# Weights decoded by one product, a shift and two merges, with the first two units on VectorE, and new orders in the first and the last head pairs

## The chip, the cores and the metric

The kernel runs on one core of a Trainium2 chip. The metric is the device time of one execution in microseconds (us). The kernel before takes 601.79 us, the median of three runs (601.74 to 602.01). Its profiled execution took 602.28 us. From its first to its last instruction that execution spans 600.4 us.

## The reference

Attention with a soft cap, then two feed-forward layers. In short:

```python
q, k, v: [2, 12, 448, 64] float32          # 2 batches, 12 heads
s = cap * tanh((q @ k.T / 8) / cap)
a = softmax(s) @ v                          # -> x: [896, 768]
h = x @ w_in;  g = h * sigmoid(1.702 * h);  y = g @ w_out      # 768 -> 2048 -> 768
yn = y / sqrt(mean(y*y) + 1e-6) * rms_g
out = (silu(yn @ w_gate) * (yn @ w_val)) @ w_out2              # 768 -> 1536 -> 768
```

The five weight matrices are float64. The kernel therefore reads each weight as two 32-bit words, `lo` and `hi`, and makes the float32 number from them on the chip. The float64 exponent has 11 bits and a bias of 1023, the float32 exponent has 8 bits and a bias of 127.

## The kernel before

**Arithmetic.** Every matrix product whose precision matters is made of three: a number is split into a high part that TensorE takes in its fast format (float32r) and the rest, and the products high-high, high-rest and rest-high are added in PSUM.

**Attention.** There are 12 *pairs* of heads, p = 0 to 11. A pair has three full key chunks (c = 0, 1, 2) for both heads, and one chunk of the last 64 keys of both heads together (c = 3, "last"). Per pair:

- VectorE splits q and k (`split_kq`, L253 and L254), two pairs ahead.
- TensorE makes the scores (L272, 6 products for each chunk; L280, 3 for the last). A chunk of scores takes one of three PSUM buffers. The last chunk, the outputs and the sums take turns in two others.
- ScalarE takes tanh (L299) and exp (L302), in place, in tiles `pa` (chunks 0, 1) and `pb` (chunks 2, 3).
- TensorE makes the outputs (L318, 32 products of a quarter each) and the sums of the probabilities (L362). The sums are fed by streams: chunk 1 for pairs below 4, then `ts`, which is a sum of two or three chunks, then the last chunk. For pairs below 4 `ts` is one addition on GpSimd (L346); from pair 4 on VectorE adds two chunks first (L340) and GpSimd the third.
- VectorE copies the outputs from PSUM (`copy_out`, L330) and takes the reciprocals of the sums (L367). Both free a PSUM buffer that TensorE needs for the next pair.
- The reciprocals go through DRAM (`keep_recips`, `spread`) and come back spread over the partitions; for the last three pairs a product with `sel` spreads them (L383). Five pairs later VectorE multiplies and splits the result (`norm_mul`, `norm_hi`, `norm_lo`).

The code is written out in the order in which each engine gets its work; nothing else reorders it. In pass p of the loop stand the scores of pair p (chunks 1, 2), then chunk 0 of pair p+1, the last chunk of p, and behind them the outputs and sums of pair p-1.

**Weights.** A *unit* is 128 x 768 weights, and there are 68. SyncE's queue loads a unit's words into `raw` (three buffers); a load for unit w+3 waits until unit w is decoded (`low`). Unit by unit, `open_`, then the decoding, then a split into two parts in `ring` (`high_part`, `low_part`). From unit 2 on ScalarE makes a mask in three instructions (`square`, `sign`, `mask`), VectorE puts the exponent and mantissa under it (`mid`), merges the sign and top bits (`top`) and the three bits of `lo` (`low`). Units 0 and 1 are decoded during attention: ScalarE takes the absolute value (`size`), VectorE limits it and shifts (`clip`, `field`), then `top` and `low`; `plan_a` and `plan_d` say in which pass each of these stands.

**Feed-forward.** Columns of 18 products (`group`, L580 to L582) run unit by unit, and `tick` and `ahead` place the decoding of later units behind them. All eight PSUM banks then belong to one pool, so the first column takes over a bank that attention had used.

Of the kernel before, what the change touches and what calls it, by code (L numbers as in the profile page):

```python
# [8 lines left out]
F32 = mybir.dt.float32  # L9
F32R = mybir.dt.float32r  # L10
U32 = mybir.dt.uint32
AF = mybir.ActivationFunctionType
# [5 lines left out]
def attn_moe_kernel(  # L18
# [24 lines left out]
    NC = 3  # L43
# [5 lines left out]
    def f(ap):  # L49
        return ap.bitcast(F32)  # L50
# [1 line left out]
    keep = ctx.enter_context(tc.tile_pool(name="keep", bufs=1))  # L52
    capt = keep.tile([128, 1], F32, name="capt")
    tsc = keep.tile([128, 1], F32, name="tsc")
    edge = keep.tile([128, 1], F32, name="edge")
    blk = keep.tile([128, 128], F32, name="blk")
    ones = keep.tile([128, 128], F32R, name="ones")
    sel = keep.tile([128, 64], F32, name="sel")
# [63 lines left out]
        dec_t[w] = (d, r[:, :, 0], r[:, :, 1])  # L122
        return dec_t[w]

    def size(w):
        d, lo, hi = open_(w)
        nc.scalar.activation(out=f(d), in_=f(hi), func=AF.Abs)

    def clip(w):
        d = dec_t[w][0]  # L130
        nc.vector.tensor_scalar(out=f(d), in0=f(d), scalar1=2.0 ** -15, scalar2=None, op0=ALU.max)

    def field(w):
        d = dec_t[w][0]
        nc.vector.tensor_scalar(
            out=d, in0=d, scalar1=3, scalar2=0x3FFFFFFF, op0=ALU.logical_shift_left, op1=ALU.bitwise_and
        )

    def square(w):
        d, lo, hi = open_(w)  # L140
        nc.scalar.activation(out=f(d), in_=f(hi), func=AF.Square, scale=2.0 ** 15)  # L141

    def sign(w):
        d = dec_t[w][0]
        nc.scalar.activation(out=f(d), in_=f(d), func=AF.Sign, bias=edge)  # L145

    def mask(w):
        d = dec_t[w][0]
        nc.scalar.activation(out=f(d), in_=f(d), func=AF.Relu, scale=2.0 - 2.0 ** -23)  # L149

    def mid(w):
        d, lo, hi = dec_t[w]
        nc.vector.scalar_tensor_tensor(  # L153
            out=d, in0=hi, scalar=3, in1=d, op0=ALU.logical_shift_left, op1=ALU.bitwise_and
        )

    def top(w):
        d, lo, hi = dec_t[w]
        nc.vector.scalar_tensor_tensor(  # L159
            out=d, in0=hi, scalar=0xC0000000, in1=d, op0=ALU.bitwise_and, op1=ALU.bitwise_or  # L160
        )

    def low(w):
# [7 lines left out]
    def high_part(w):  # L171
        ring = pools["ring0" if w % 6 < 3 else "ring1"]
        t = ring.tile([128, 2, 768], F32R, tag="ring", name="ring")
        nc.scalar.activation(out=t[:, 0], in_=f(dec_t[w][0]), func=AF.Copy)  # L174
        wt[w] = t

    def low_part(w):
# [5 lines left out]
            done.add((op, w))  # L183
            op(w)

    ACT_OPS, DVE_OPS = (square, sign, mask), (mid, top, low)

    def block(u0, i):
        w = wt[u0 + i // 6]
# [3 lines left out]
    def attention():  # L193
        with ExitStack() as actx:
# [145 lines left out]
                nc.vector.tensor_tensor(out=ts_[p], in0=pa[p][:, 0], in1=pa[p][:, 1], op=ALU.add)  # L340

            def add_third(p):
                eng = nc.gpsimd if p < NPR - 1 else nc.vector
                if p < THREE:
                    ts_[p] = ap_.tile([128, 2, S], F32, tag="ts", name="ts")
                eng.tensor_tensor(  # L346
                    out=ts_[p], in0=pa[p][:, 0] if p < THREE else ts_[p], in1=pb[p][:, 0:2], op=ALU.add
                )

            def sums(p):  # L350
                ps = ps_v.tile([128, 512], F32, tag="v", name="v")
                streams = [pa[p][:, 1]] if p < THREE else []
                streams += [ts_[p], None]
# [12 lines left out]
                nr[p] = zrp.tile([128, SH], F32, tag="rs", name="rs", bufs=4)  # L366
                nc.vector.reciprocal(out=nr[p], in_=ps[:, 0:SH])  # L367
# [73 lines left out]
            plan_a = {  # L441
                1: [(size, 0)], 2: [(size, 1)], 3: [(high_part, 0)], 5: [(high_part, 1)],
                12: [(square, 2), (sign, 2), (mask, 2)],
            }
            plan_d = {
                1: [(clip, 0), (field, 0)], 2: [(top, 0), (low, 0)], 3: [(clip, 1), (field, 1)],
                4: [(low_part, 0), (top, 1)], 5: [(low, 1)], 7: [(low_part, 1)],
            }

            def decode(plan, p):  # L450
# [1 line left out]
                    run(*op)  # L452

            split_first(ts, x)

            for p in range(NPR + 1):
                load_kq(p + 3)
# [19 lines left out]
                elif p < NPR:  # L477
                    tanh(p, 0)
                    scores(p, 1)
                    tanh(p, 1)  # L480
                    scores(p, 2)
                    tanh(p, 2)
                    scores(p + 1, 0)
                    scores_last(p)
                    tanh(p, NC)
                    exp(pa[p])
                    exp(pb[p])
                    decode(plan_a, p)
                else:
                    decode(plan_a, p)  # L490
                if 3 <= p < NPR:
# [5 lines left out]
                decode(plan_d, p)  # L497
                if p < NPR:
                    add_two(p)
                if p == 1:  # L500
                    outputs(0, (2, NC))
                elif p:
                    outputs(p - 1)
                if NPR - 1 <= p:
                    spread_late(p - 2)
                if p:
                    if p < NPR:
                        copy_out(p - 1, "D")
                    sums(p - 1)
                    if p < NPR - 2:  # L510
                        keep_recips(p - 1)
                if p < NPR:
                    add_third(p)
                if NPR - 3 <= p < NPR:
# [1 line left out]
                if p == NPR:  # L516
                    copy_out(p - 1, "A")
                    some = (p - 3, p - 2, p - 4)
                    for step in (norm_mul, norm_hi, norm_lo):
                        for q_ in some:  # L520
                            step(q_)
            return spread_product, norm_mul, norm_hi, norm_lo

    def rest(spread_product, norm_mul, norm_hi, norm_lo):
        with ExitStack() as fctx:
# [29 lines left out]
            def ahead(u):  # L555

                return (
                    [(high_part, u + 3), (square, u + 5), (mid, u + 4), (top, u + 4)],
                    [(sign, u + 5), (mask, u + 5), (low, u + 4), (low_part, u + 3)],
                )  # L560


# [63 lines left out]
            for c in range(NC1):  # L626
# [18 lines left out]
                for n, (i, b) in enumerate(order):  # L645
                    last = ()
                    if c == 0 and n == 0:
                        later(lambda: spread_product(q3, [bank()[:, 0:B * S // 4] for _ in range(2)]))
                        later(lambda: norm_mul(q3), lambda: norm_hi(q3), lambda: run(mid, 2), lambda: norm_lo(q3))
# [207 lines left out]
            while due:  # L857
                tick(lambda: None)

    nc.vector.memset(edge, -0.99)  # L860
    nc.vector.memset(f(ones), 1.0)
    with tc.manual_schedule():
        tail = attention()
# [65 lines left out]
```

## Time and profile before

| what | value |
| --- | --- |
| median of three runs | 601.79 us |
| profiled execution, and its span | 602.28 us, 600.4 us |
| TensorE busy (PE) | 586.3 us, 98% |
| VectorE busy (DVE) | 445.7 us, 74% |
| ScalarE busy (ACT) | 388.6 us, 65% |
| GpSimd busy (POOL) | 66.1 us, 11% |
| mean granted TensorE clock | 0.996 of full speed |

"Busy" is time in which an instruction is in the engine. Shares over the whole span mix two stages. Attention fills the first 102 us and the two feed-forward layers the rest. In a timeline a row gives start, length, engine, line, instruction (output <- inputs) and count; a bracket gives the engine's idle time ahead of it and what ended that. An instruction that does not need the one ahead of it on its engine starts a little before that one's end, so lengths overlap by some 0.08 us; the chain of waits counts each stretch of time once.

### The profile page before, as it was taken

The numbers are of one execution on the slowest core, as the hardware profiler recorded it, in microseconds if no ns is written. First come the engines' busy times: TensorE is split into PE (matmuls) and PEld (weight loads), VectorE is DVE, ScalarE is ACT, GpSimd is POOL, SyncE is SP. The second block draws the span as 40 slices with busy tenths as digits, with TensorE's granted clock in tenths as the row PEclk, the third lists the DMA queues.
The fourth block names the chain that finished last, engine by engine and source line by source line (L and its number), as shares of the span: only waits on it lengthen the run. The fifth ranks groups of instructions, "written<-read, shape, count | busy, mean of one in ns | idle before, by whom it ended". The sixth has DMA issues, their size and how long they took to land.

```text
span 600.4 us, 8518 instructions
## 1 busy us (share of the span) xinstructions
PE 586.3 (98%) x3417; PEld 499.9 (83%) x3417; DVE 445.7 (74%) x548; ACT 388.6 (65%) x507; POOL 66.1 (11%) x52
## 2 busy tenths in 40 slices
PE   7899998999999999999999999999999999999997
PEld 4354554898899888888889888899999999999997
DVE  5578998798665446666878899995588896688842
ACT  6989996799756457777667666674455582466400
POOL 1312240000000000000022203200022100122100
PEclk9899999999999999999999999999999999999999
DMA  8265420254342413334324134342333342233012
GB/s 295 99 221 164 144 69 21 87 176 143 119 145 77 149 53 105 106 106 131 121 89 134 60 98 154 110 131 81 101 111 105 106 158 86 73 105 106 1 79 106
DMA packets 54450, 67.93 MB, mean 113 GB/s; under 512 B 2918, under 2 KB 49162, under 8 KB 54410
## 3 DMA queue, kind: packets, MB, share of 16 engines
q1 hardware_dynamic: 54122, 67.15, 34.1%
q8 instruction: 27, 0.44, 0.3%
q10 hardware_dynamic: 288, 0.23, 0.1%
q14 instruction: 13, 0.11, 0.1%
HBM read 64.59 MB, written 2.78 MB: 112 GB/s over the span
## 4 chain that ended last, share of the span: by engine, by line
PE 91%; DVE 4%; ACT 3%; issue 1%; DMA 1%; SPq 0%; DVEq 0%
PE b L582 23%; PE b L581 23%; PE b L580 23%; PE b L790 15%; PE v L318 5%; PE s L272 2%; PE v L362 1%; DVE rs L367 1%; ACT pa L302 1%; PE v L280 1%; ACT pb L302 1%; DMA first<-in_k 1%; ACT pa L299 1%; ACT pb L299 1%; DVE ts L340 1%
## 5 line engine op out<-in xcount | busy, mean ns | idle before, releaser
L580 PE MATMUL b<-x,ring 128*128 128x512 f32 (+1 forms) x480 | 174.0, 362 | 2.2 <-DVE z L401 2.2
L582 PE MATMUL b<-x,ring 128*128 128x512 f32 (+1 forms) x480 | 174.3, 363 | 0.0
L581 PE MATMUL b<-x,ring 128*128 128x512 f32 (+1 forms) x480 | 174.1, 363 | 0.0
L580 PEld LDWEIGHTS b<-x,ring 128*128 128x128 f32 x480 | 90.1, 188 | 12.7 <-DVE z L401 2.6
L581 PEld LDWEIGHTS b<-x,ring 128*128 128x128 f32 x480 | 90.1, 188 | 9.9
L582 PEld LDWEIGHTS b<-x,ring 128*128 128x128 f32 x480 | 90.1, 188 | 9.4
L790 PE MATMUL b<-ring,uA 128*128 128x384 f32 x504 | 87.8, 334 | 0.0
L790 PEld LDWEIGHTS b<-ring,uA 128*128 128x128 f32 x504 | 87.4, 188 | 0.0
L153 DVE SCALAR_TENSOR_TENSOR dec<-raw,dec 128x768 uint32<-128x768 uint32 x66 | 67.8, 1028 | 24.7 <-ACT dec L149 23.4
L159 DVE SCALAR_TENSOR_TENSOR dec<-raw,dec 128x768 uint32<-128x768 uint32 x68 | 73.3, 1077 | 1.1
L179 DVE TENSOR_TENSOR ring<-dec,ring 128x768 fp32r<-128x768 f32 x68 | 66.8, 984 | 4.6 <-ACT ring L174 4.6
L582 PE MATMUL b<-g,ring 128*128 128x384 f32 (+1 forms) x192 | 70.0, 365 | 0.0
L581 PE MATMUL b<-g,ring 128*128 128x384 f32 (+1 forms) x192 | 69.9, 364 | 0.0
L580 PE MATMUL b<-g,ring 128*128 128x384 f32 (+1 forms) x192 | 69.6, 362 | 0.0
L165 DVE SCALAR_TENSOR_TENSOR dec<-raw,dec 128x768 uint32<-128x768 uint32 x68 | 64.9, 955 | 3.7 <-ACT ring L174 2.3
L174 ACT ACTIVATE ring<-dec 128x768 fp32r<-128x768 f32 x68 | 56.7, 834 | 16.4 <-DVE dec L165 8.2
L145 ACT ACTIVATE dec<-dec,edge 128x768 f32<-128x768 f32 x66 | 61.5, 932 | 1.0
L141 ACT ACTIVATE dec<-raw 128x768 f32<-128x768 f32 x66 | 59.2, 897 | 0.5 <-DVE ring L179 0.5
L149 ACT ACTIVATE dec<-dec 128x768 f32<-128x768 f32 x66 | 55.6, 843 | 1.5
L758 POOL TENSOR_TENSOR a<-a,gg 128x512 f32<-128x512 f32 (+1 forms) x18 | 29.6, 1645 | 188.6 <-DVE gg L751 188.6
L761 ACT ACTIVATE uA<-a 128x512 fp32r<-128x512 f32 (+1 forms) x24 | 13.9, 578 | 46.3 <-POOL a L758 34.5
L612 DVE TENSOR_TENSOR g<-gg,g 128x384 fp32r<-128x384 f32 (+1 forms) x32 | 20.0, 625 | 27.3 <-ACT g L609 27.1
(95 smaller groups left out, 640.1 us busy)
## 6 DMA issues: line engine op xcount, KB each, us to landing
raw<-in_moe_w_out SPq DMA_DIRECT2D x20, 768.0 KB
raw<-in_moe_w_in SPq DMA_DIRECT2D x16, 768.0 KB
raw<-in_moe_w_gate SPq DMA_DIRECT2D x12, 768.0 KB
raw<-in_moe_w_val SPq DMA_DIRECT2D x12, 768.0 KB
raw<-in_moe_w_out SPq DMA_DIRECT2D x8, 512.0 KB
v<-in_v SPq DMA_DIRECT2D x12, 256.0 KB
kq<-in_k SPq DMA_DIRECT2D x11, 256.0 KB
kq<-in_q SPq DMA_DIRECT2D x11, 224.0 KB
```

Source lines behind the costliest of these rows:

```text
L141: nc.scalar.activation(out=f(d), in_=f(hi), func=AF.Square, scale=2.0 ** 15)
L145: nc.scalar.activation(out=f(d), in_=f(d), func=AF.Sign, bias=edge)
L149: nc.scalar.activation(out=f(d), in_=f(d), func=AF.Relu, scale=2.0 - 2.0 ** -23)
L153: nc.vector.scalar_tensor_tensor(out=d, in0=hi, scalar=3, in1=d, op0=ALU.logical_shift_left, op1=ALU.bitwise_and)
L159: nc.vector.scalar_tensor_tensor(out=d, in0=hi, scalar=0xC0000000, in1=d, op0=ALU.bitwise_and, op1=ALU.bitwise_or)
L165: nc.vector.scalar_tensor_tensor(out=d, in0=lo, scalar=29, in1=d, op0=ALU.logical_shift_right, op1=ALU.bitwise_or)
L174: nc.scalar.activation(out=t[:, 0], in_=f(dec_t[w][0]), func=AF.Copy)
L179: nc.vector.tensor_tensor(out=t[:, 1], in0=f(d), in1=f(t[:, 0]), op=ALU.subtract)
L580: nc.tensor.matmul(out=wide(o, b), lhsT=w0, rhs=x0, start=first, stop=False)
L581: nc.tensor.matmul(out=wide(o, b), lhsT=w0, rhs=x1, start=False, stop=False)
L582: nc.tensor.matmul(out=wide(o, b), lhsT=w1, rhs=x0, start=False, stop=last)
L790: nc.tensor.matmul(out=os_[t][n][:, 0:HW], lhsT=uA[xi][:, i, tok], rhs=w[:, wi, n * HW:(n + 1) * HW], start=(i == 0 and xi == 0 and wi == ...
```

## The change

1. **Decoding.** The `hi` word, read as a float32, is multiplied by 2^-112 (`scale`). Read so, its exponent field is the float64 exponent divided by 8, and 896 = 8 x 112 is the difference of the two biases. Shifted left by three (`shift`) the product holds the float32 exponent and 20 bits of mantissa. `top` merges the sign alone, and `low` the last three bits as before. `square`, `sign`, `mask`, `mid`, `size`, `clip`, `field` and the constant `edge` go.
2. **Units 0 and 1** are scaled, and their high part is copied, on VectorE. ScalarE has no decoding left before pass 12. The passes change: unit 0 in passes 1 and 2, unit 1 in passes 2 to 4 (before: to pass 7).
3. **Passes 1 and 2**: ScalarE takes `exp(pa)` before the last chunk's tanh, and the outputs and sums of the pair before stand ahead of the last chunk's scores and the next pair's chunk 0. VectorE's copy and reciprocal come ahead of `split_kq` and the decoding.
4. **Pair 0** has its sums fed by four streams, without an addition on GpSimd.
5. **Pass 12**: the multiplications of pairs 8 and 9 stand ahead of the last reciprocal.

```diff
+    def scale(w):
         d, lo, hi = open_(w)
+        if w < 2:
+            nc.vector.tensor_scalar(out=f(d), in0=f(hi), scalar1=2.0 ** -112, scalar2=None, op0=ALU.mult)
+        else:
+            nc.scalar.activation(out=f(d), in_=f(hi), func=AF.Copy, scale=2.0 ** -112)
+
+    def shift(w):
         d = dec_t[w][0]
+        nc.vector.tensor_scalar(out=d, in0=d, scalar1=3, scalar2=None, op0=ALU.logical_shift_left)
...
-            out=d, in0=hi, scalar=0xC0000000, in1=d, op0=ALU.bitwise_and, op1=ALU.bitwise_or
+            out=d, in0=hi, scalar=0x80000000, in1=d, op0=ALU.bitwise_and, op1=ALU.bitwise_or
...
-        nc.scalar.activation(out=t[:, 0], in_=f(dec_t[w][0]), func=AF.Copy)
+        if w < 2:
+            nc.vector.tensor_copy(t[:, 0], f(dec_t[w][0]))
+        else:
+            nc.scalar.activation(out=t[:, 0], in_=f(dec_t[w][0]), func=AF.Copy)
...
-    ACT_OPS, DVE_OPS = (square, sign, mask), (mid, top, low)
+    ACT_OPS, DVE_OPS = (scale,), (shift, top, low)
...
-                1: [(clip, 0), (field, 0)], 2: [(top, 0), (low, 0)], 3: [(clip, 1), (field, 1)],
-                4: [(low_part, 0), (top, 1)], 5: [(low, 1)], 7: [(low_part, 1)],
+                1: [(scale, 0), (shift, 0), (top, 0), (low, 0)], 2: [(high_part, 0), (low_part, 0), (scale, 1)],
+                3: [(shift, 1), (top, 1)], 4: [(low, 1), (high_part, 1), (low_part, 1)],
...
-                    [(high_part, u + 3), (square, u + 5), (mid, u + 4), (top, u + 4)],
-                    [(sign, u + 5), (mask, u + 5), (low, u + 4), (low_part, u + 3)],
+                    [(high_part, u + 3), (scale, u + 5), (shift, u + 4), (top, u + 4)],
+                    [(low, u + 4), (low_part, u + 3)],
```

TensorE in pass 1 and the start of pass 2, before: `s` are scores, `v` the buffers of last chunks, outputs and sums.

```order
L272 MATMUL s<-x 128x448 x18
L280 MATMUL v<-x 128x448 x3
L318 MATMUL v<-pb,v 32x448 x8
L362 MATMUL v<-pa,ones 32x224 x4
L362 MATMUL v<-ts,ones 32x224 x4
L362 MATMUL v<-pb,blk 32x224 x4
L272 MATMUL s<-x 128x448 x18
L280 MATMUL v<-x 128x448 x3
L318 MATMUL v<-pa,v 32x448 x8
```

The same place now:

```order
L253 MATMUL s<-x 128x448 x12
L299 MATMUL v<-pb,v 32x448 x8
L347 MATMUL v<-pa,ones 32x224 x8
L347 MATMUL v<-pb,ones 32x224 x4
L347 MATMUL v<-pb,blk 32x224 x4
L261 MATMUL v<-x 128x448 x3
L253 MATMUL s<-x 128x448 x18
L299 MATMUL v<-pa,v 32x448 x8
L299 MATMUL v<-pb,v 32x448 x8
```

The rest of pair 0's outputs (`v<-pb,v`) and its sums (L347) have moved ahead of the last chunk of pair 1 and of chunk 0 of pair 2, and the stream of `ts` is now two streams of `pa` and `pb`.

VectorE in passes 1 and 2, before: `kq` is the raw pair that is split, `z` the copied outputs, `rs` the reciprocals, `dec` and `raw` belong to a weight unit.

```order
L131 TENSOR_SCALAR dec<-dec 128x768
L135 TENSOR_SCALAR dec<-dec 128x768
L330 COPY z<-v 128x448
L367 RECIPROCAL rs<-v 128x224
L253 CAST x<-kq 128x960
L254 TENSOR_TENSOR x<-kq,x 128x960
L159 SCALAR_TENSOR_TENSOR dec<-raw,dec 128x768
L165 SCALAR_TENSOR_TENSOR dec<-raw,dec 128x768
L330 COPY z<-v 128x448
L367 RECIPROCAL rs<-v 128x224
L253 CAST x<-kq 128x960
L254 TENSOR_TENSOR x<-kq,x 128x960
```

The same place now:

```order
L311 COPY z<-v 128x448
L352 RECIPROCAL rs<-v 128x224
L234 CAST x<-kq 128x960
L235 TENSOR_TENSOR x<-kq,x 128x960
L127 TENSOR_SCALAR dec<-raw 128x768
L133 TENSOR_SCALAR dec<-dec 128x768
L137 SCALAR_TENSOR_TENSOR dec<-raw,dec 128x768
L143 SCALAR_TENSOR_TENSOR dec<-raw,dec 128x768
L311 COPY z<-v 128x448
L352 RECIPROCAL rs<-v 128x224
L234 CAST x<-kq 128x960
L235 TENSOR_TENSOR x<-kq,x 128x960
```

The copy and the reciprocal of pair 0 wait for no decoding any more, four instructions of unit 0 stand together behind the split of pair 3, and the copy of pair 1 stands behind these four.

VectorE at the end of attention, before: `late` is a PSUM buffer with spread reciprocals, the product `z<-z,r` is pair 8's.

```order
L410 CAST x_65<-z 128x448
L417 TENSOR_TENSOR x_66<-z,x_65 128x448
L367 RECIPROCAL rs<-v 128x224
L401 TENSOR_TENSOR z<-z,late 128x448 x2
L398 TENSOR_TENSOR z<-z,r 128x448
L417 TENSOR_TENSOR x_66<-z,x_65 128x448 x3
```

The same place now:

```order
L395 CAST x_64<-z 128x448
L402 TENSOR_TENSOR x_65<-z,x_64 128x448
L383 TENSOR_TENSOR z<-z,r 128x448
L386 TENSOR_TENSOR z<-z,late 128x448
L352 RECIPROCAL rs<-v 128x224
L386 TENSOR_TENSOR z<-z,late 128x448
L402 TENSOR_TENSOR x_65<-z,x_64 128x448 x3
```

The products of pair 8 and of pair 9 (the first with `late`) have moved ahead of the last reciprocal, and only that of pair 10 is left behind it.

## Rows read from the trace of the kernel before

**Rows 1.** Windows: stretch, length; busy PE, PEld, DVE, ACT, POOL; PEclk, DMA, GB/s
```profile
13.30:31.20 17.90, 13.62 (x127) 6.34 (x128) 8.43 (x9) 15.52 (x16) 6.47 (x3) 0.90 0.42 143
...
52.15:88.27 36.12, 34.17 (x351) 17.75 (x347) 34.07 (x42) 32.74 (x32) 10.67 (x6) 1.00 0.41 127
...
101.90:597.00 495.10, 495.00 (x2532) 453.06 (x2532) 367.03 (x449) 303.57 (x424) 41.35 (x28) 1.00 0.32 105
```

**Rows 2.** Timeline, 12 to 32 us: start, length, engine, line, instruction, idle before
```profile
12.29 1.42 ACT L302 ACTIVATE pb<-pb,capt 128x1344 f32<-128x1344 f32 x1
...
20.07 2.09 POOL L346 TENSOR_TENSOR ts<-pa,pb 128x896 f32<-128x896 f32 x1 [4.12 <-ACT pb L302]
...
20.83 1.75 DVE L131 TENSOR_SCALAR dec<-dec 128x768 f32<-128x768 f32 x1 [7.77 <-ACT dec L127]
...
22.61 0.56 DVE L135 TENSOR_SCALAR dec<-dec 128x768 uint32<-128x768 uint32 x1
...
23.76 0.88 PE L280 MATMUL v<-x 128*128 128x448 f32 x3 [1.14 <-DVE z L330]
...
25.09 0.60 DVE L253 CAST x<-kq 128x960 fp32r<-128x960 f32 x1
...
25.72 1.16 DVE L254 TENSOR_TENSOR x<-kq,x 128x960 fp32r<-128x960 f32 x1
25.89 0.40 SPq L217 DMA_DIRECT2D kq<-in_k  x1
...
26.79 0.95 DVE L159 SCALAR_TENSOR_TENSOR dec<-raw,dec 128x768 uint32<-128x768 uint32 x1
...
27.78 0.96 DVE L165 SCALAR_TENSOR_TENSOR dec<-raw,dec 128x768 uint32<-128x768 uint32 x1
```

**Rows 3.** Chain that ended last: start, length, engine, tile, line, count
```profile
25.22 4.91 PE v L318 x32
...
31.27 2.02 PE s L272 x18
33.29 0.82 PE v L280 x3
34.10 3.15 PE v L318 x32
37.25 1.13 PE v L362 x24
...
53.70 1.00 DVE ts L340
54.70 0.54 DVE z L330
55.24 1.46 DVE rs L367
...
74.08 0.76 PE v L362 x16
```

**Rows 4.** Timeline, pairs 6 to 11
```profile
52.15 2.39 PE L272 MATMUL s<-x 64*128 64x448 f32 x18
...
52.74 0.96 DVE L165 SCALAR_TENSOR_TENSOR dec<-raw,dec 128x768 uint32<-128x768 uint32 x1 [2.29 <-ACT ring L174]
...
66.86 0.95 DVE L179 TENSOR_TENSOR ring<-dec,ring 128x768 fp32r<-128x768 f32 x1
...
88.27 1.50 PE L272 MATMUL s<-x 64*128 64x448 f32 x12
```

**Rows 5.** Timeline, end of attention and first product behind it
```profile
98.71 0.62 DVE L417 TENSOR_TENSOR x<-z,x 128x448 fp32r<-128x448 f32 x1
...
99.84 1.56 DVE L367 RECIPROCAL rs<-v 128x224 f32<-128x224 f32 x1 [0.51 <-PE v L362]
101.32 1.09 DVE L401 TENSOR_TENSOR z<-z,late 128x448 f32<-128x448 f32 x2
...
101.93 0.44 PE L580 MATMUL b<-x,ring 128*128 128x384 f32 x1 [2.16 <-DVE z L401]
```

More of the change, by code (lines that the diff above doesn't have):

```diff
@@ L54, in attn_moe_kernel @@
     tsc = keep.tile([128, 1], F32, name="tsc")
-    edge = keep.tile([128, 1], F32, name="edge")
     blk = keep.tile([128, 128], F32, name="blk")
@@ L123, in open_ @@
         return dec_t[w]
-    def size(w):
+    def scale(w):
         d, lo, hi = open_(w)
-        nc.scalar.activation(out=f(d), in_=f(hi), func=AF.Abs)
-    def clip(w):
-        d = dec_t[w][0]
[L131 to L155, printed above, removed]
+        if w < 2:
[3 more added lines that the diff above has]
+    def shift(w):
+        d = dec_t[w][0]
+        nc.vector.tensor_scalar(out=d, in0=d, scalar1=3, scalar2=None, op0=ALU.logical_shift_left)
     def top(w):
@@ L342, in add_third @@
             def add_third(p):
+                if p == 0:
+                    return
                 eng = nc.gpsimd if p < NPR - 1 else nc.vector
@@ L351, in sums @@
                 ps = ps_v.tile([128, 512], F32, tag="v", name="v")
-                streams = [pa[p][:, 1]] if p < THREE else []
-                streams += [ts_[p], None]
+                if p == 0:
+                    streams = [pa[p][:, 0], pa[p][:, 1], pb[p][:, 0:2], None]
+                else:
+                    streams = [*([pa[p][:, 1]] if p < THREE else []), ts_[p], None]
                 for n, some in enumerate(streams):
@@ L439, in attention @@
                 nc.tensor.matmul(out=warm[:, 0:S], lhsT=ones, rhs=xA[0][:, 0, 0:S], start=True, stop=True)
[L441 to L444, printed above, removed]
+            plan_a = {12: [(scale, 2)]}
             plan_d = {
-                1: [(clip, 0), (field, 0)], 2: [(top, 0), (low, 0)], 3: [(clip, 1), (field, 1)],
-                4: [(low_part, 0), (top, 1)], 5: [(low, 1)], 7: [(low_part, 1)],
+                1: [(scale, 0), (shift, 0), (top, 0), (low, 0)], 2: [(high_part, 0), (low_part, 0), (scale, 1)],
+                3: [(shift, 1), (top, 1)], 4: [(low, 1), (high_part, 1), (low_part, 1)],
             }
@@ L454, in attention, with products @@
             split_first(ts, x)
+            EARLY = 3
+            def products(p):
+                outputs(p, range(NC + 1) if p else (2, NC))
+                if p + 1 >= NPR - 1:
+                    spread_late(p - 1)
+                if p < NPR - 1:
+                    copy_out(p, "D")
+                sums(p)
             for p in range(NPR + 1):
@@ L482, in attention @@
                     tanh(p, 2)
-                    scores(p + 1, 0)
-                    scores_last(p)
+                    if p < EARLY:
+                        exp(pa[p])
+                        products(p - 1)
+                        scores_last(p)
+                        scores(p + 1, 0)
+                    else:
+                        scores(p + 1, 0)
+                        scores_last(p)
                     tanh(p, NC)
-                    exp(pa[p])
+                    if p >= EARLY:
+                        exp(pa[p])
                     exp(pb[p])
-                    decode(plan_a, p)
                 else:
@@ L499, in attention @@
                     add_two(p)
[L500 to L511, printed above, removed]
+                if p == NPR:
+                    norm_mul(p - 4)
+                    norm_mul(p - 3)
+                if p >= EARLY:
+                    products(p - 1)
+                if 1 <= p < NPR - 2:
+                    keep_recips(p - 1)
                 if p < NPR:
@@ L518, in attention @@
                     some = (p - 3, p - 2, p - 4)
-                    for step in (norm_mul, norm_hi, norm_lo):
+                    norm_mul(p - 2)
+                    for step in (norm_hi, norm_lo):
                         for q_ in some:
@@ L648, in rest @@
                         later(lambda: spread_product(q3, [bank()[:, 0:B * S // 4] for _ in range(2)]))
-                        later(lambda: norm_mul(q3), lambda: norm_hi(q3), lambda: run(mid, 2), lambda: norm_lo(q3))
+                        later(lambda: norm_mul(q3), lambda: norm_hi(q3), lambda: run(shift, 2), lambda: norm_lo(q3))
                         last = (
```

1 line of the change is left out of this document (removed).

## The prediction

> **What bounds the kernel now.** I read the stretches first, then the timeline of the waiting engines, then the chain of waits. From 101.9 us to 597 us TensorE is busy 495.00 of 495.10 us [rows 1]: the feed-forward layers are bound by TensorE alone, and nothing that the change does to ScalarE and VectorE there can win more than 0.1 us. What can be won lies in attention. TensorE idles 4.3 us from 13.3 to 31.2 and 1.95 us from 52.15 to 88.27 [rows 1], and 2.16 us where attention hands over [rows 5]. In the first of these stretches ScalarE is busy 15.5 of 17.9 us [rows 1], and the waits end with VectorE: a last chunk waits 1.14 us for a copy out of PSUM [rows 2] that stood behind `clip` and `field`. The outputs of pair 1 behind these waits then take 4.91 us where those of pair 2 take 3.15 [rows 3]. The granted clock of that stretch is 0.90, so part of it ran at the lower level, 1.2 GHz: 1.76 us more.
>
> TensorE's own work for a pair is 2.02 of scores, 0.82 of last chunk, 3.15 of outputs and 1.13 of sums, 7.12 us; from pair 4 on the sums take 0.76, and a pair 6.75 us [rows 3].
>
> **The early pairs.** Up to exp of pair 0's `pb`, which ends at 12.29 + 1.42 = 13.71 [rows 2], nothing is moved. Now the rest of pair 0's outputs comes next, half of 3.15, then four streams of sums at 1.13/3 each: 13.71 + 1.58 + 1.51, with some 0.1 of hand-offs, and VectorE's reciprocal of pair 0 can start at 16.9. From there VectorE has everything in one row, in the order shown, up to the reciprocal of pair 3, and never has to wait for data that is not long there. The terms:
>
> - 4 reciprocals at 1.46, 3 copies at 0.54, one addition of 1.00 [rows 3]: 8.46.
> - 4 splits, from the start of a cast to the start of what follows, 26.79 - 25.09 = 1.70 [rows 2]: 6.80.
> - 4 merges (`top`, `low`, two units), start to start 27.78 - 26.79 = 0.99 [rows 2]: 3.96.
> - 2 `low_part` at 0.95 [rows 4]: 1.90.
> - 2 `scale`, 2 `shift`, 2 copies into the ring, all with one source of 768 numbers, at the 0.56 of `field` [rows 2]: 3.36.
> - GpSimd's additions for pairs 1, 2 and 3. While one of 2.09 us ran, a `clip` of VectorE took 1.75 us, and it ended 0.42 after GpSimd [rows 2]; its neighbour `field` of the same size took 0.56. So the two engines exclude each other. VectorE has here no gap in which such an addition could hide except beside work from PSUM, so I take 2.09 for each: 6.27.
>
> The sum is 30.75, and the reciprocal of pair 3 ends at 47.65. The outputs of pair 4 need its buffer; 3.15 + 0.76 later, with a hand-off of 0.1, the scores of pair 6 start at 51.7. Before they start at 52.15 [rows 4]. **The gain so far is only 0.45 us**: TensorE's waits move from ScalarE and `clip` to a VectorE that is full. Two of them stay: before the last chunk of pair 2 (its own work done at about 23.9, the copy of pair 1 at 25.8, by the same terms), and before the last chunk of pair 4 (37.6; the copy of pair 2 at 39.0). In the first the clock may fall again, but outputs 2 are done some 4 us before VectorE reaches their copy, which covers 1.76.
>
> On the exclusion the Trainium skill, SBUF — State Buffer, "Who interferes with whom", says that a VectorE instruction with two SBUF inputs, or in a mode that takes two ports, and a GpSimd instruction that reads SBUF hold a shared pair of ports in turn, the later one blocked. It is the rule that speaks most against putting decoding on VectorE beside these additions; the `clip` row agrees, and the 6.27 stands by the row.
>
> ScalarE loses two `size` and two `high_part` in early pairs; it stops being the limit there, and its new order only serves the outputs. SyncE's queue now issues three weight loads together in pass 1, and that of unit 3 waits for `low` of unit 0, at 25.3 by the terms. Behind it stand pair 0's reciprocals and the loads of pair 5; the latter were issued at 25.89 before [rows 2] and come at about 26 now, 7 us before their split: nothing. `scale` reads every second word. If that made it as slow as a merge, 0.96 [rows 2], two of them add 0.8; from below they can't be under 0.56. On this the Trainium skill, VectorE: DVE Perf Modes, "Mode 2×_2P — use both read ports for one tensor", asks for one SBUF source and an even outermost dimension, not for neighbouring words, so by it both keep 0.56 and the sum stays; by the merge's row the time would be 0.8 more. No row here shows the form.
>
> **Pairs 6 to 11.** No decoding is left after pass 4. From 52.15 to 88.27 five pairs take 36.12 us, against 5 x 6.75 = 33.75. The 2.37 are the two places where VectorE was late: `low` of unit 1 waited 2.29 us for ScalarE's `high_part`, and `low_part` of unit 1 took 0.95 [rows 4]. Both go. What is late next is TensorE itself: VectorE was busy 34.07 in this stretch, 32.2 without these two, 6.4 a pair, under 6.75. The scores of pair 11 then start at 51.7 + 33.75 = 85.45, **2.8 us earlier** than 88.27.
>
> **The hand-over.** TensorE is done with attention at 101.93 - 2.16 = 99.77 and waits for the last reciprocal and then for the product that reads `late`, whose bank the first column takes [rows 5]. This product now stands ahead of the reciprocal. The subtraction before it ends at 98.71 + 0.62 = 99.33; two products at 1.09/2 each [rows 5] end at 100.4, and the column starts at 100.5: **1.4 us**. The reciprocal starts 0.6 later than before; its readers are the spread product and the second column, 3 us on.
>
> **Feed-forward.** Three ScalarE instructions and a merge per unit become one and a `shift` of 0.56. TensorE's own work hides it: 0. From above the gain is the 0.1 idle; from below I take one more wait like the longest on VectorE in these rows, 2.16, which no row suggests.
>
> **Sum.** 2.8 + 1.4 = 4.2: 602.28 - 4.2 = 598.1 for the profiled execution, and, as that stands 0.49 over the median, **597.6 us** for the median.
>
> **Rivals.**
>
> *The additions hide (B).* If GpSimd's three additions fall beside copies and reciprocals, 6.27 goes from the chain. TensorE's own work is then the bound: from 16.9 three pairs at 7.12, one at 6.75 and another last chunk and chunk 0 (1.5), so pair 6 starts at 46.5, 5.2 earlier: 592.4. For it: additions run beside reciprocals in later pairs. Against: in passes 1 to 3 they become ready while VectorE is splitting.
>
> *VectorE dearer, and a low clock (C).* `scale` at 0.96 adds 0.8. If the clock falls at the second wait, near pair 4, where no slack covers it, 1.76 more: 597.6 + 2.6 = 600.2. For it: the clock did fall after waits of this kind. Against: those waits were longer together.
>
> *VectorE the bound for good, slower (D).* If each of the six one-source instructions pays as the blocked `clip` does, 1.75, on top of the three blocks, that is 6 x 1.19 = 7.1: pair 6 starts at 58.8, and the time is 604.7. It decides from 4.2 us more on VectorE in passes 1 to 4. Against: GpSimd has only three additions there.
>
> **Chances.** Forecast 0.55 (its own range 596.2 to 599.2), B 0.12, C 0.24, D 0.05, and 0.04 for something else near no change. The measurement can tell 0.2%, 1.2 us, from no change. B and the forecast are faster, of C two thirds, and the rest of C is the same: faster 0.84, same 0.11, slower 0.05. The range of 594.5 to 600.6 leaves out the far half of B, D and what lies beyond C.
>
> **What would show it.** In the changed profile: TensorE's longest waits in early pairs end with VectorE's copy (L311), at 25 to 26 and at 38 to 39 us; one-source decoding instructions at 0.56, some blocked to 2 us or more by GpSimd; pair 6's scores at 51.7; pairs from there at 6.75; the first column 0.7 us behind the last sums and ahead of the last reciprocal's end; from there 495 us to the end of TensorE. I am wrong if pair 6 starts under 49 or over 53, or if TensorE idles over 1 us in the feed-forward layers.

## The result, and the profile after

The changed kernel takes **596.28 us** (median of four runs, 595.70 to 596.45), the kernel before 601.90 beside it. The ratio is 0.990, with an interval of 0.989 to 0.992. The prediction was 597.6 us. Its sign held, and its mechanism in the main; two of its terms had the wrong size, in opposite directions. The experiments then showed something that it had not considered: one part of the change costs two microseconds.

The profiled execution took 596.45 us with a span of 594.7. The stretches of its time, as in [rows 1]:

```profile
core 0: us, PE busy (x) PEld busy (x) DVE busy (x) ACT busy (x) POOL busy (x), PEclk, DMA share, GB/s
13.30:31.20 17.90, 14.57 (x156) 8.25 (x155) 14.38 (x14) 15.42 (x16) 4.13 (x2) 1.00 0.64 208
31.20:50.00 18.80, 18.80 (x207) 9.47 (x207) 18.52 (x23) 17.41 (x17) 5.23 (x3) 1.00 0.63 189
50.00:82.60 32.60, 32.60 (x329) 17.69 (x331) 29.93 (x38) 31.01 (x30) 10.60 (x5) 1.00 0.37 116
96.00:591.20 495.20, 495.00 (x2532) 453.06 (x2532) 340.56 (x449) 198.16 (x294) 38.06 (x28) 1.00 0.33 105
```

From 96 us on TensorE is busy 495.00 of 495.20 us, as it was 495.00 of 495.10 before, while ScalarE's busy time there fell from 303.57 to 198.16 us. From 31.2 us to the end of attention TensorE no longer idles. TensorE's starts at the places of the sum (the last chunk with the longest wait and the scores behind it, the scores of pairs 6 and 11, the first feed-forward column; start, length, and in brackets the wait ahead):

```profile
26.11 0.87 PE L261 MATMUL v<-x 128*128 128x448 f32 x3 [1.81 <-DVE z L311]
26.91 2.10 PE L253 MATMUL s<-x 64*128 64x448 f32 x18
30.05 0.87 PE L253 MATMUL s<-x 64*128 64x448 f32 x6 [1.03 <-ACT pa L280]
49.79 2.11 PE L253 MATMUL s<-x 64*128 64x448 f32 x18
83.49 1.50 PE L253 MATMUL s<-x 64*128 64x448 f32 x12
96.17 0.45 PE L574 MATMUL b<-x,ring 128*128 128x384 f32 x1 [1.17 <-DVE z L386]
```

Before, these were 52.15 for pair 6 and 88.27 for pair 11 [rows 4], and 101.93 for the first column [rows 5]. So the gain is:

| stretch | before | after | gain | predicted |
| --- | --- | --- | --- | --- |
| to the scores of pair 6 | 52.15 | 49.79 | 2.36 | 0.45 |
| pair 6 to pair 11 | 36.12 | 33.70 | 2.42 | 2.37 |
| pair 11 to the first column | 13.66 | 12.68 | 0.98 | 1.4 |
| feed-forward, TensorE busy | 495.00 | 495.00 | 0 | 0 |

VectorE in the early pairs, from the reciprocal of pair 0 to that of pair 3, as far as it shows what GpSimd does to it (L127 is `scale`, L160 `low_part`, L137 `top`):

```profile
17.24 1.56 DVE L352 RECIPROCAL rs<-v 128x224 f32<-128x224 f32 x1 [0.89 <-PE v L347]
20.42 2.50 DVE L127 TENSOR_SCALAR dec<-raw 128x768 f32<-128x768 f32 x1
29.73 2.75 DVE L160 TENSOR_TENSOR ring<-dec,ring 128x768 fp32r<-128x768 f32 x1
32.41 0.55 DVE L127 TENSOR_SCALAR dec<-raw 128x768 f32<-128x768 f32 x1
35.22 0.96 DVE L137 SCALAR_TENSOR_TENSOR dec<-raw,dec 128x768 uint32<-128x768 uint32 x1
36.10 0.62 DVE L311 COPY z<-v 128x448 f32<-128x448 f32 x1
36.63 1.55 DVE L352 RECIPROCAL rs<-v 128x224 f32<-128x224 f32 x1
43.81 1.55 DVE L352 RECIPROCAL rs<-v 128x224 f32<-128x224 f32 x1
```

And GpSimd's three additions in that time:

```profile
20.39 2.11 POOL L329 TENSOR_TENSOR ts<-pa,pb 128x896 f32<-128x896 f32 x1 [18.20 <-ACT pb L283]
29.18 2.48 POOL L329 TENSOR_TENSOR ts<-pa,pb 128x896 f32<-128x896 f32 x1 [6.68 <-ACT pb L283]
35.51 2.65 POOL L329 TENSOR_TENSOR ts<-pa,pb 128x896 f32<-128x896 f32 x1 [3.85 <-issue]
```

Lay the two over each other. The first addition ran from 20.39 to 22.50, and `scale`, which takes 0.55 at 32.41, took 2.50. The second made `low_part` take 2.75 instead of 0.96. The third came while a merge was running: this time GpSimd's row is the long one (2.65), and what VectorE did after the merge, a copy and a reciprocal, both read from PSUM and took no longer than elsewhere.

### The profile page after: what moved, and what is told of

Same layout as the page of the kernel before. It is cut to its first block, busy times and chain, and to the rows that moved or that the text cites. A ratio compares the mean times of both kernels' runs of the same rounds, so it can differ in the third digit from the quotient of the medians.

```text
span 594.7 us, 8421 instructions
## 1 busy us (share of the span) xinstructions
PE 584.2 (98%) x3425; PEld 500.5 (84%) x3425; DVE 421.2 (71%) x549; ACT 278.5 (47%) x371; POOL 61.5 (10%) x51
## 4 chain that ended last, share of the span: by engine, by line
PE 84%; DMA 6%; DVE 6%; issue 1%; ACT 1%; SPq 0%
PE b L576 23%; PE b L575 23%; PE b L574 23%; PE b L784 15%; DMA r<-recs 4%; DMA recs<-rs 1%; DVE rs L352 1%; DVE x L235 1%; DMA first<-in_k 1%; DMA kq<-in_k 1%; DVE x L234 1%; DVE ts L321 1%; DVE z L311 1%; DVE dec L127 1%; DVE z L383 0%
## 5 line engine op out<-in xcount | busy, mean ns | idle before, releaser
L160 DVE TENSOR_TENSOR ring<-dec,ring 128x768 fp32r<-128x768 f32 x68 | 68.6, 1010 | 23.3 <-ACT ring L155 18.2
L137 DVE SCALAR_TENSOR_TENSOR dec<-raw,dec 128x768 uint32<-128x768 uint32 x68 | 73.2, 1076 | 1.2
L155 ACT ACTIVATE ring<-dec 128x768 fp32r<-128x768 f32 x66 | 55.3, 838 | 35.2 <-DVE dec L143 24.3
L143 DVE SCALAR_TENSOR_TENSOR dec<-raw,dec 128x768 uint32<-128x768 uint32 x68 | 64.9, 955 | 1.4
L752 POOL TENSOR_TENSOR a<-a,gg 128x512 f32<-128x512 f32 (+1 forms) x18 | 26.3, 1462 | 191.5 <-DVE gg L745 183.0
L133 DVE TENSOR_SCALAR dec<-dec 128x768 uint32<-128x768 uint32 x68 | 42.4, 624 | 0.0
L575 PEld LDWEIGHTS b<-g,ring 128*128 128x128 f32 x192 | 36.0, 188 | 4.0
L574 PEld LDWEIGHTS b<-g,ring 128*128 128x128 f32 x192 | 36.1, 188 | 4.0
```

Of the source, the lines that this page charges most:

```text
L133: nc.vector.tensor_scalar(out=d, in0=d, scalar1=3, scalar2=None, op0=ALU.logical_shift_left)
L137: nc.vector.scalar_tensor_tensor(out=d, in0=hi, scalar=0x80000000, in1=d, op0=ALU.bitwise_and, op1=ALU.bitwise_or)
L143: nc.vector.scalar_tensor_tensor(out=d, in0=lo, scalar=29, in1=d, op0=ALU.logical_shift_right, op1=ALU.bitwise_or)
L160: nc.vector.tensor_tensor(out=t[:, 1], in0=f(d), in1=f(t[:, 0]), op=ALU.subtract)
L574: nc.tensor.matmul(out=wide(o, b), lhsT=w0, rhs=x0, start=first, stop=False)
L575: nc.tensor.matmul(out=wide(o, b), lhsT=w0, rhs=x1, start=False, stop=False)
```

## The experiments

The theory T: the gain is made in attention alone, in the three places of the table, and VectorE, blocked by GpSimd, is the limit of passes 1 to 4. Rivals: the lighter decoding in the feed-forward layers gives the gain (R1), or the new orders of passes 1 and 2 give nothing, and only the removed waits for ScalarE and `clip` count (R2). The kernel before took 602.1 to 603.1 us in the medians beside these runs, single runs 601.8 to 603.6; ratios are to those. In five of the profiles (runs 2, 7, 8, 11 and 12 below) sixteen of the first products took some 3.35 us instead of 2.01, so starts are compared from the next place that this does not reach.

**1. New decoding in the feed-forward layers only (the kernel before with it).**

```diff
...
-    ACT_OPS, DVE_OPS = (square, sign, mask), (mid, top, low)
+    ACT_OPS, DVE_OPS = (scale,), (shift, top, low)
...
```

> The kernel before, with the new decoding (one product on ScalarE, shift, two merges) for units 2 and later only; everything in attention stays as before except that one unit's first step in pass 12 is one instruction instead of three. Theory T (the whole gain of 5.5 us is made in attention; in the feed-forward stretch TensorE alone is the limit, busy 495.00 of 495.20 us): 601.5 to 602.2 us, scores of pair 6 at 52.15 and of pair 11 at 88.27 as before, ScalarE's busy time down by some 110 us. Rival R1 (the lighter decoding in the feed-forward layers gives the gain or most of it): 596 to 598.5 us.

602.77 us, ratio 1.000 (0.999 to 1.001). That is 0.6 above T's window, but the kernel before was up beside it too (602.90).

**2. The reverse, the changed kernel with the old decoding from unit 2 on.**

> The changed kernel, with the old decoding (square, sign, mask on ScalarE, mid on VectorE) for units 2 and later; attention keeps the new decoding of units 0 and 1 and the new orders. T: 596.0 to 596.8 us, pair 6 at 49.8, feed-forward 495.0 us. R1: 600 to 602 us.

596.74 us, ratio 0.990 (0.989 to 0.991), that of the changed kernel. The stretch from 96 us, first of 1, then of 2:

```profile
96.00:595.00 499.00, 496.84 (x2573) 452.73 (x2566) 343.52 (x453) 198.92 (x295) 38.07 (x28) 1.00 0.32 104
```

```profile
96.00:595.00 499.00, 495.00 (x2532) 453.09 (x2532) 369.00 (x451) 303.52 (x424) 41.07 (x28) 1.00 0.32 106
```

ScalarE is busy 199 us in the one and 304 in the other; in the second, whose feed-forward layers lie wholly in this stretch, TensorE's 495.00 us stay. (In the first it also holds the end of attention. Run 1 keeps the waits of before: 2.6 us for ScalarE, 2.2 at the hand-over.) R1 falls, twice.

**3. The old hand-over.**

```diff
-                if p == NPR:
-                    norm_mul(p - 4)
-                    norm_mul(p - 3)
...
-                    norm_mul(p - 2)
-                    for step in (norm_hi, norm_lo):
+                    for step in (norm_mul, norm_hi, norm_lo):
```

> The changed kernel, with the products of pairs 8 and 9 back behind the last reciprocal in pass 12. T: the hand-over's 1.0 us goes: first feed-forward column some 2.1 us behind the last sums instead of 1.17, 597.0 to 597.6 us; nothing else moves. Rival (the product waits for its DMA of reciprocals anyway, so the place does not matter): within 0.3 us of 596.3.

599.01 us, ratio 0.994 (0.992 to 0.995): more than T's upper end. The waits of TensorE (us in total, times, longest) and the early stretch of the profiled execution (598.17 us):

```profile
PE b L570 <- DVE z L386: 2.2, 1, 2.2
PE v L261 <- DVE z L311: 1.9, 1, 1.9
```

```profile
13.30:31.20 17.90, 15.43 (x156) 8.79 (x152) 14.22 (x14) 15.41 (x16) 3.95 (x2) 0.91 0.60 197
```

```profile
27.09 4.54 PE L253 MATMUL s<-x 64*128 64x448 f32 x24
```

The first column starts 2.16 us behind the sums, not 1.17: the 1.0 is there. The other 0.7 was there at pair 6 already, at 50.49 (0.15 of it a later start). Nothing differs in the code of these passes; but after the wait of 1.85 us for VectorE's copy the granted clock fell, to 0.91 over the stretch, so that part of it ran at 1.2 GHz, and 24 products of scores took 4.54 us where the changed kernel had 2.10 + 0.87 and a wait of 1.03. With the same instructions up to there and the same wait the clock falls in two of the profiled executions (this one, and run 6 with 0.90) and stays at 1.00 in two others (the changed kernel's and run 2's). How often it falls is not known. The profiled execution is the fastest of the five; where the other four, at 598.78 to 599.18, lose 0.6 to 1.0 us more is not shown.

**4. The old order of scores, exp and outputs in passes 1 and 2.**

```diff
-            EARLY = 3
+            EARLY = 1
```

This brings back the order of all three engines: on VectorE too, copy and reciprocal of passes 1 and 2 stand behind the split and the decoding again.

> The changed kernel, with the old order of scores, exp and outputs in passes 1 and 2 (scores of the next pair ahead of the outputs of the pair before); the new decoding on VectorE, the four streams of pair 0 and pass 12 stay. T has VectorE as the limit of early pairs from the first reciprocal on, and the old order makes that reciprocal start at 20 to 21 us instead of 17.2 because the outputs and sums of pair 0 stand behind 3 us of scores: pair 6 at 51.5 to 53, 598 to 600 us. Rival R2 (the orders give nothing; only the removal of the waits for ScalarE and clip counts): 596.0 to 596.8 us, pair 6 at 49.8.

**594.07 us**, ratio 0.986 (0.984 to 0.987): 2.2 us *faster* than the changed kernel. Both expectations missed; T had the sign wrong, and R2, by which the orders are worth nothing, was 2 us off. Pair 6 starts at 47.74. TensorE's waits, VectorE and GpSimd in early pairs:

```profile
PE s L253 <- ACT pa L280: 1.4, 1, 1.4
PE b L574 <- DVE z L386: 0.7, 1, 0.7
```

```profile
14.27 0.56 DVE L127 TENSOR_SCALAR dec<-raw 128x768 f32<-128x768 f32 x1 [1.01 <-DMA raw<-in_moe_w_in]
20.99 1.74 DVE L234 CAST x<-kq 128x960 fp32r<-128x960 f32 x1
25.79 0.62 DVE L311 COPY z<-v 128x448 f32<-128x448 f32 x1
26.93 1.56 DVE L352 RECIPROCAL rs<-v 128x224 f32<-128x224 f32 x1 [0.51 <-PE v L347]
32.91 0.62 DVE L311 COPY z<-v 128x448 f32<-128x448 f32 x1 [1.25 <-PE v L299]
34.04 1.56 DVE L352 RECIPROCAL rs<-v 128x224 f32<-128x224 f32 x1 [0.51 <-PE v L347]
```

```profile
20.10 2.12 POOL L329 TENSOR_TENSOR ts<-pa,pb 128x896 f32<-128x896 f32 x1 [17.90 <-ACT pb L283]
26.31 2.13 POOL L329 TENSOR_TENSOR ts<-pa,pb 128x896 f32<-128x896 f32 x1 [4.10 <-ACT pb L283]
33.48 2.12 POOL L329 TENSOR_TENSOR ts<-pa,pb 128x896 f32<-128x896 f32 x1 [5.04 <-ACT pb L283]
```

Two things differ. In the old order VectorE decodes unit 0 from 14.27 on, when it has nothing else to do, and not behind the first reciprocal. And exp of `pb`, which releases GpSimd, ends a little behind the outputs of the pair before (for the second addition at 26.24 and 25.73), so the second and third addition run beside a reciprocal from PSUM; only the first blocks VectorE, by 1.1 us (a cast of 1.74 instead of 0.60). TensorE waits once, 1.40 us from 13.3 on; in the changed kernel 0.48, 1.81 and 1.03. The difference of 1.92 is nearly the difference of the distance from the scores of pair 1 to those of pair 6 (9.75 to 47.74, and 10.00 to 49.79: 1.80).

**5. No addition on GpSimd for pairs 1 and 2** (four streams instead of three).

```diff
+            FOUR = 3
...
-                if p == 0:
+                if p < FOUR:
```

> The changed kernel, with the sums of pairs 1 and 2 fed by four streams as those of pair 0, so that GpSimd's two additions at 20.39 and 29.18 us, beside which a product took 2.50 us and a subtraction 2.75 us on VectorE, are not there. Theory T (VectorE, blocked by GpSimd, is the limit of passes 1 to 4 in the new order): VectorE's row is 1.9 + 1.8 = 3.7 us shorter, TensorE has 2 x 0.38 = 0.76 more to do and becomes the limit: scores of pair 6 at 47.3 to 48.3 instead of 49.79, 594.0 to 595.2 us. Rival (the blocking is not what holds the early pairs; the place of copy and reciprocal in the order is): only the 0.76 shows, pair 6 at 50 to 50.6, 596.5 to 597.2 us.

594.73 us, ratio 0.988 (0.986 to 0.989), pair 6 at 48.44. T's time came; pair 6 is 0.14 past its window. VectorE's `scale` and `low_part` take 0.55 and 0.96 again, and the wait of 1.81 for the copy is gone:

```profile
20.20 0.55 DVE L127 TENSOR_SCALAR dec<-raw 128x768 f32<-128x768 f32 x1
28.29 0.96 DVE L160 TENSOR_TENSOR ring<-dec,ring 128x768 fp32r<-128x768 f32 x1
28.32 0.87 PE L253 MATMUL s<-x 64*128 64x448 f32 x6 [1.05 <-ACT pa L280]
```

So the blocking is what holds the early pairs in the new order. TensorE's wait of 1.03 us for ScalarE stays (1.05, last row): it belongs to the order itself. With the 0.48 ahead of it, it comes to about the 1.40 of the old order, so that the 1.81 for the copy is nearly the whole difference. Pair 6 is 0.70 later than in run 4, and the two added streams are 2 x 0.38 = 0.76 of work for TensorE: without the blocking the new order costs nothing that shows.

**6. The product of pair 9 ahead of that of pair 8 in pass 12.**

```diff
-                    norm_mul(p - 4)
                     norm_mul(p - 3)
+                    norm_mul(p - 4)
```

> The changed kernel, with the product of pair 9 (the one that frees the bank of the first column) ahead of that of pair 8 in pass 12. T (the product of pair 8 waited 0.40 us for its reciprocals from DRAM and then took 0.54 ahead of the one that mattered): first column 0.2 us behind the last sums instead of 1.17, 595.1 to 595.6 us. Rival (the product of pair 9 is itself late): 596.0 to 596.5 us.

595.65 us, ratio 0.989 (0.987 to 0.990), and the column starts 0.15 us behind the sums instead of 1.17. Against the changed kernel the ratios alone do not separate 0.6 us; the trace does, since the wait at that place is gone (and 0.35 of the 1.0 is lost to a later start and the clock before pair 6).

**7. The changed kernel's orders with units 0 and 1 decoded as before.**

```diff
...
-                1: [(scale, 0), (shift, 0), (top, 0), (low, 0)], 2: [(high_part, 0), (low_part, 0), (scale, 1)],
-                3: [(shift, 1), (top, 1)], 4: [(low, 1), (high_part, 1), (low_part, 1)],
+                1: [(clip, 0), (field, 0)], 2: [(top, 0), (low, 0)], 3: [(clip, 1), (field, 1)],
+                4: [(low_part, 0), (top, 1)], 5: [(low, 1)], 7: [(low_part, 1)],
```

> The changed kernel's orders (passes 1, 2 and 12, four streams for pair 0) and its decoding from unit 2 on, but units 0 and 1 decoded as before: size and the high part on ScalarE, clip, field, merges and low part on VectorE in the passes of before. T (with the new order VectorE is the limit of passes 1 to 4; the old places take 3 to 4 us of work off it there and give the late stalls back): pair 6 at 47.5 to 50, then 36.1 instead of 33.7 us to pair 11, 596 to 598.5 us. Rival (moving the decoding is what makes the early pairs faster): pair 6 at 51.5 to 53, 599 to 601.5 us.

598.81 us, ratio 0.994 (0.993 to 0.996). It lies between the two expectations: pair 6, at 51.24, is later than T had it and earlier than the rival. From there to pair 11 it takes 36.09 us, as in the kernel before. The late stalls are thus those of unit 1's old decoding. The early part is not clean: 0.9 of its 51.24 is a later start (scores of pair 2 at 18.79, not 17.91), and the granted clock was 0.69 from 32 to 36 us. Two additions block VectorE here too:

```profile
21.86 1.93 DVE L137 TENSOR_SCALAR dec<-dec 128x768 f32<-128x768 f32 x1 [0.46 <-ACT dec L133]
28.43 2.84 DVE L151 SCALAR_TENSOR_TENSOR dec<-raw,dec 128x768 uint32<-128x768 uint32 x1
```

**8. Unit 0's decoding ahead of the copy, all else as changed.**

```diff
                         exp(pa[p])
+                        if p == 1:
+                            decode(plan_d, 1)
                         products(p - 1)
...
-                decode(plan_d, p)
+                if p != 1:
+                    decode(plan_d, p)
```

> The changed kernel, with one thing moved: on VectorE in pass 1 the four decoding instructions of unit 0 stand ahead of the copy of pair 0's outputs instead of behind the split of pair 3. The orders of TensorE and ScalarE stay new. Theory T2 (what the new order costs is on VectorE: it sat idle 4.09 us before that copy, and 3.0 us of decoding that had its data from 14.2 us on then lay behind the reciprocal, in the row that limits passes 1 to 4): scores of pair 6 at 47.5 to 48.3 instead of 49.79, 594.2 to 595.0 us. Rival (the order of TensorE itself, outputs and sums ahead of the scores, is what costs the 2.2 us against the old order): pair 6 at 49.4 or later, 595.9 to 596.8 us.

597.12 us, ratio 0.991 (0.990 to 0.993): no gain, and 0.3 past the rival's window. From the scores of pair 2, at 18.70, to pair 6, at 50.44, it takes 31.74 us, the changed kernel 31.88. T2 was wrong that the place of these 3.0 us is enough. VectorE:

```profile
24.00 0.62 DVE L311 COPY z<-v 128x448 f32<-128x448 f32 x1 [2.70 <-PE v L299]
28.32 2.46 DVE L153 CAST ring<-dec 128x768 fp32r<-128x768 f32 x1
34.51 2.82 DVE L137 SCALAR_TENSOR_TENSOR dec<-raw,dec 128x768 uint32<-128x768 uint32 x1
```

By the scores of pair 3 1.91 us were won (7.09 instead of 9.00 behind those of pair 2); 1.73 of it was lost again between 34.82 and 43.66, where the changed kernel needs 7.11 us for the same scores, outputs and sums: the third addition now fell on a merge (2.82), where it had fallen on reads from PSUM. So it is the meeting of additions and decoding, set by the order of TensorE and ScalarE, that costs.

**9 to 12. On from run 4.** Pass 12 as in run 6 (9); that, and two streams instead of three for pairs 2 and 3, `THREE = 2` (10); that, and the read of the reciprocals (`spread`) a pass earlier (11), or at the head of its own pass (12):

```diff
-            THREE = 4
+            THREE = 2
```

Run 11, which also has four buffers for the read instead of three, and run 12:

```diff
-                if 3 <= p < NPR:
-                    spread(p - 3)
+                if 2 <= p < NPR - 1:
+                    spread(p - 2)
```

```diff
             for p in range(NPR + 1):
+                if 3 <= p < NPR:
+                    spread(p - 3)
                 load_kq(p + 3)
                 load_v(p + 2)
...
-                if 3 <= p < NPR:
-                    spread(p - 3)
```

> The kernel with the old order in passes 1 and 2 (594.07 us), with the product of pair 9 ahead of that of pair 8 and nothing else. T: the idle 0.68 us ahead of the first column shrinks to 0.1: 593.3 to 593.7 us. Rival: the product of pair 9 is late itself, 594.0.

> The kernel with the old order in passes 1 and 2 (594.07 us), where TensorE is without a wait from 14.6 us to the end of attention; with the product of pair 9 ahead of that of pair 8, and the sums of pairs 2 and 3 from two streams (VectorE adds two chunks, GpSimd the third) instead of three. T (TensorE's own work is now the limit, so what shortens it shows whole): 2 x 0.38 = 0.76 less in pairs 2 and 3 and 0.55 of idle time less at the hand-over, 592.6 to 593.1 us. Rival (two more additions of 1.0 us make VectorE the limit again): 594 to 596 us with waits for the copy in pairs 3 to 5.

> The kernel with the old order, two streams for pairs 2 and 3 and the product of pair 9 first (593.96 us, where five products on VectorE waited 3.1 us in all for the reciprocals that are read back from DRAM, the longest of these reads landing 13.33 us after its issue), with the read of a pair's reciprocals issued one pass earlier, into four buffers instead of three. T (TensorE's row is 0.76 us shorter in early pairs and the loss behind it is this DMA's lateness): no wait for these reads up to pair 11, pairs 6 to 11 at 6.74 each, 592.4 to 593.0 us. Rival (the waits are VectorE's own load, or the read is no earlier for being issued earlier, because the queue waits for the write ahead of it): 593.6 to 594.5 us.

> The kernel with the old order, two streams for pairs 2 and 3 and the product of pair 9 first (593.96 us), with the read of a pair's reciprocals issued at the head of its pass, ahead of the loads of k, q and v instead of behind them: about 1.5 us earlier, its data written a pass ago, and with nothing of these loads in front of it. T (the read was late because 0.7 MB of loads went through ahead of it): VectorE's waits for these reads, 3.1 us in all, go, pairs 6 to 11 take 6.74 us each, 592.5 to 593.2 us. Rival (the loads of k and q, now behind the read, become late, as they did when the read was issued a pass earlier): VectorE waits for these loads instead, 594 to 596 us.

| run | us | ratio, interval | pair 6 | pair 6 to 11 |
| --- | --- | --- | --- | --- |
| 4 | 594.07 | 0.986, 0.984 to 0.987 | 47.74 | 33.72 |
| 9 | 593.81 | 0.985, 0.984 to 0.987 | 47.71 | 34.03 |
| 10 | 593.96 | 0.986, 0.985 to 0.987 | 47.21 | 34.82 |
| 11 | 596.51 | 0.990, 0.989 to 0.991 | 48.01 | 38.12 |
| 12 | 598.70 | 0.993, 0.992 to 0.994 | 50.20 | 36.83 |

The profiles of 11 and 12 start later (their scores of pair 3 come at 27.79 and 27.38, those of runs 4, 9 and 10 at 26.77 to 26.99), and the one of 11 took 598.05 us; for these two only the last column compares.

Run 9 starts its first column 0.26 us earlier than run 4 (93.38 instead of 93.64), and its time lies 0.1 over T's window and 0.2 under the rival. Run 10 missed T's time. It wins 0.5 us before pair 6 and gives it back. In its chain of waits the longest piece of attention behind pair 6 is one DMA, and VectorE waits for such reads, 3.1 us in all (in run 9 2.8):

```profile
58.24 13.33 DMA r<-recs
```

```profile
71.59 0.63 DVE L383 TENSOR_TENSOR z<-z,r 128x448 f32<-128x448 f32 x1 [1.05 <-DMA r<-recs]
```

Moving the read did not help. VectorE's waits for it between pairs 6 and 11 are gone in both runs, but in run 11 its issue waits on SyncE for the write ahead of it (first row), with the loads of q and k queued behind; in run 12 it hardly waits (0.5 us in all), but goes ahead of these loads. In both VectorE then waits for the loads (second row: run 11; third: run 12; us in total, times, longest):

```profile
SPq L362 <- DMA recs<-rs: 36.6, 7, 6.3
```

```profile
DVE x L234 <- DMA kq<-in_q: 5.4, 6, 1.9
```

```profile
DVE x L234 <- DMA kq<-in_q: 6.6, 6, 3.0
```

For 11 and 12 the rival's mechanism was right, but the times lie beyond its windows too, by 2.0 and 2.7 us. As both moves made the loads late, it stays open whether the reads are what costs run 10 its gain. Run 9, at 593.81, is the fastest of the kernels, but not told apart from 4 and 10.

## Why the prediction was right, and where not

The sums of the prediction come out as they stand, but for the chances: 0.55, 0.12 and two thirds of 0.24 are 0.83 for faster, not 0.84, and 0.12 is left for the same, not 0.11.

**The feed-forward layers: 0.** Right; runs 1 and 2 show it from both sides.

**Pairs 6 to 11: 2.37.** Right, 2.42; run 7 has 36.09 with unit 1's old places. In the changed profile VectorE is busy 29.93 of the 32.60 us from 50.00 to 82.60, and TensorE all of it.

**The early pairs: 0.45.** They gave 2.36. The mechanism was right in the main, one term was too large, and the last link did not hold. VectorE did run in one row from 17.24 to 45.36 (predicted: 16.9 to 47.65), and the last chunk of pair 2 waited for the copy, 1.81 us up to 26.11 (predicted: a copy at 25.8). The row is 28.1 us, not 30.75. The term "three additions at 2.09, 6.27" is what failed: two cost 2.50 - 0.55 = 1.95 and 2.75 - 0.96 = 1.79, the third nothing, 3.74 in all, which is 2.53 of the 2.63 missing. The case was told as rival B, but all or nothing; it came true for one addition of three. The argument against B, that the additions "become ready while VectorE is splitting", was not worked out addition by addition: the third became ready during the merge right ahead of a copy and a reciprocal. The row of the blocked `clip` showed that the engines exclude each other. Where they do not was open in the trace of the kernel before, in later pairs, where an addition and a reciprocal run side by side at their usual lengths:

```profile
61.48 2.12 POOL L346 TENSOR_TENSOR ts<-ts,pb 128x896 f32<-128x896 f32 x1 [4.51 <-DVE ts L340]
61.76 1.55 DVE L367 RECIPROCAL rs<-v 128x224 f32<-128x224 f32 x1
```

The Trainium skill, SBUF — State Buffer, "Who interferes with whom", says which kinds meet: VectorE with two SBUF inputs or in a mode of two ports does, with at most one SBUF input outside those modes does not. The copy of 0.62 and the reciprocal of 1.55 beside the third addition agree.

With the row shorter the second predicted wait, at 38 to 39 us, is not there, and pair 6 came at 49.79 instead of 51.7. The link that failed is the one from VectorE's row to pair 6: the prediction lets the outputs of pair 4 wait for the reciprocal of pair 3. This reciprocal ends at 45.36, and the outputs start behind TensorE's own last chunk, without a wait:

```profile
45.89 1.71 PE L299 MATMUL v<-pa,v 128*32 128x448 f32 x16
```

From 30.05 on TensorE's own work brings it to 49.79; by the predicted link the measured row would give 45.36 + 3.15 + 0.76 + 0.1 = 49.4. TensorE's last wait, the 1.03 us ahead of 30.05, is for ScalarE, of which the prediction says that it stops being the limit and which has no term in its sum; before, 2.6 of the 4.3 us that TensorE idled there were waits for ScalarE.

`scale` with its stride took 0.55, so the dearer half of rival C did not happen; a low clock did, at the first wait and not at the second, in runs 3 and 6 but not in the profile after.

**The hand-over: 1.4.** It gave 0.98. The subtraction and the two products came in the order assumed, but the product of pair 8 waited 0.40 us for a DMA that was not in the sum:

```profile
94.96 0.62 DVE L383 TENSOR_TENSOR z<-z,r 128x448 f32<-128x448 f32 x1 [0.40 <-DMA r<-recs]
95.50 0.61 DVE L386 TENSOR_TENSOR z<-z,late 128x448 f32<-128x448 f32 x1
```

This is the cost that the prediction asked about for steps before ("what is late next") and left out here: when TensorE comes earlier, a read that does not come earlier with it is late. In run 2's profile, where attention is the same, the product did not wait, and the column started 0.67 us behind the sums, as predicted (0.7):

```profile
96.62 0.44 PE L593 MATMUL b<-x,ring 128*128 128x384 f32 x1 [0.67 <-DVE z L405]
```

Run 6 takes the wait out of the way. That 597.6 came within 1.3 us of the time is in part luck: 1.9 us too little gain in the early pairs and 0.4 too much here have opposite signs.

**What the prediction took as given:** that the new order of passes 1 and 2 helps or is harmless. It costs some 2 us (run 4). The rest of the change, without these orders, gains 8.0 us. How much of that is the decoding's own is not shown: the four streams of pair 0, which take one addition from GpSimd, were in every run with the changed attention and were not tried alone.

## What to carry to other kernels

When two engines exclude each other, lay each instruction of the one over what the other does at that moment; neither "all block" nor "all hide" is an estimate. Work with early data belongs into the idle time ahead of the engine's critical row, but a new order also moves where the exclusions fall: test order and work apart. When the engine that sets the time gets faster, look first at transfers that do not get faster with it and at what stands behind them in their queue.

## What the runs showed of the hardware

GpSimd's addition takes 2.11 us, or up to 2.65 where a VectorE instruction with SBUF sources was running at its start. A VectorE instruction with SBUF sources that starts while it runs takes up to 1.95 us more, whether it has one source (2.50 instead of 0.55) or two (2.75, 2.82 and 2.84 instead of 0.96); copies and reciprocals from PSUM took 0.62 and 1.55 beside it, as elsewhere. A read that spreads reciprocals into 224 KB landed 13.33 us after its issue (run 10). The same wait of 1.8 us left the granted clock of its stretch at 1.00 in two profiled executions and at 0.90 or 0.91 in two others.
